# Two chunks inverted one by one, x ordered on chip, four raw weight buffers

## Chip, cores and metric

One core of a Trainium2 chip runs the whole program. The metric is the device time of one execution in microseconds (us); lower is better. Times of before: 2066.8 us, the median of 3 runs (2065.63 to 2069.86).

## What is computed

Three stages in fp32. A delta-rule attention over 768 steps for 4 x 8 heads of dimension 48, a mixture of 8 experts whose weights P come from 8 rounds of row and column normalisation over all tokens, and a gated product with an output matrix:

```python
for t in range(S):
    y[:, :, t] = einsum('bhd,bhde->bhe', q[:, :, t], state)
    v_old = einsum('bhde,bhd->bhe', state, kn[:, :, t])
    state = state + bt * einsum('bhd,bhe->bhde', kn[:, :, t], v[:, :, t] - v_old)
...
P = exp(x @ w_gate - max)
for _ in range(8):
    P /= P.sum(1, keepdims=True) + 1e-09
    P /= P.sum(0, keepdims=True) + 1e-09
    P *= N / E
out = sum over e of P[:, e:e+1] * (maximum(x @ w1[e], 0) @ w2[e])
...
y = ((x @ w1) * (x @ w2) @ w3) @ w_out
```

x is 3072 tokens of 384 features; an expert has 1024 hidden units.

## The kernel before

**Attention in 12 chunks of 64 steps.** Within a chunk the recurrence becomes a triangular system: the gram matrix of the keys of each head (64 x 64) is inverted, and the chunk is then a chain of small matmuls. 32 heads of a chunk lie side by side as 16 groups on two halves of the partitions. `prep_k(c)` loads keys, takes norms and the gram; `invert(j)` inverts for the chunks 2j and 2j+1 together, on VectorE (DVE), after a 32 x 32 transpose that brings heads into the partitions; `tt_make` makes the 64 x 64 inverse from 32 x 32 blocks. `prep_q(c)` makes q times k (tile `pt`). `seq(c)` is the chain over chunks: `um` (matmul into u), `um2` (the state), `pu` (the output of the chunk).

**The first two chunks are done differently**, to start early. For j = 0 only the diagonal 16 x 16 blocks are inverted, both chunks in one go (32 x 32 tiles with two blocks), and `substitute(c)` and three rounds of matmuls (`b<-vs,xst`, then twice `b<-u,xst`, with an add on DVE after each) replace the rest of the inverse.

**Expert 0 runs under the attention.** When a chunk's output x is there, `e0(c)` runs expert 0 on its 256 tokens: 72 matmuls `b<-xr,wA` and 72 `b<-hA,wA`, each 128x256. `seq(c)` writes x from `xst` to memory (`xs_d`), `xload` reads it back in another order of rows, ScalarE (ACT) rounds it into `xr`, and GpSimd (POOL) or DVE subtracts for the low half. `load_w(n)` brings the 8 blocks of expert 0's weights through two raw buffers (`yr`, `wraw`); ACT rounds a block into `wA` and POOL subtracts 768 columns for its low half. Logits of a chunk (`b<-xr,wg`, `b<-masks,yr`) follow. Then come the normalisation, experts 1 to 7 (phase B) and the last stage (phase C), from about 423 us on.

**What sets the order.** A planner (`Plan.order`) lists all operations before anything runs, by priorities, its own costs and ring buffers; each engine's list is then fixed and worked in order. TensorE (PE) gets fillers, dummy matmuls `b<-wz`, wherever the planner sees a gap before expert 0 starts. VectorE and GpSimd instructions that the planner marks `port=True` may hold each other up. All DMAs named here are issued by SyncE (SP), one after another.

Of the kernel before, what the change touches and what calls it, by code (L numbers as in the profile page):

```python
# [7 lines left out]
F32 = mybir.dt.float32  # L8
# [41 lines left out]
SUB = 2  # L50
FLAT = "p a b c d -> p (a b c d)"
# [28 lines left out]
class Plan:  # L80
# [58 lines left out]
    WARM = 20.0  # L139
    SEED = 32  # L140
    PASS_BY = .05
# [238 lines left out]
class Kernel:  # L380
# [56 lines left out]
    def setup(self):  # L437
        nc, T, g = self.nc, self.T, self.g
        n = NCH * NG
        self.open("const", "left", ones=((128, 128), F32), masks=((128, 78), F32),  # L440
                  wgr=((128, 3, NE), F32), p=((128, NTT + 1, NE + 1), F32),
                  rs=((128, NTT), F32), cs=((128, NE), F32), sml=((128, 8), F32))
        self.open("wg", "left", wg=((128, 3, 2 * NE), F32R), padl=((128, 24), F32))
# [13 lines left out]
                  asys=((128, 1056), F32), t=((128, 1056), F32), prod=((128, NP, 1024), F32), xs=((128, 256), F32), bm2=((128, 2, 32), F32), wz=((128, 384), F16),  # L457
# [52 lines left out]
    def prep_k(self, c):  # L510
# [13 lines left out]
        if st:  # L524
            n0 = [("n0", 0), ("n0", 1)]
            bm = lambda: T["bm"][:, 32 * j:32 * j + 32]
            nv = lambda: T["nv"][:, 32 * j:32 * j + 32]
            g.op({"DVE": .1}, lambda e: nc.vector.tensor_scalar(out=nr(0), in0=nr(0), scalar1=1e-30, scalar2=None, op0=ALU.max), w=n0, prio=pr)
            g.op({"ACT": .25}, lambda e: nc.scalar.activation(out=nr(1), in_=nr(0), func=AF.Sqrt), r=n0, w=["n1"], prio=pr)

            def newton(e):
                v = nc.vector
                v.reciprocal(out=nr(2), in_=nr(1))
                v.tensor_tensor(out=nr(2), in0=nr(2), in1=nr(0), op=ALU.mult)
                v.tensor_tensor(out=nr(1), in0=nr(1), in1=nr(2), op=ALU.add)
                v.tensor_scalar(out=nv(), in0=nr(1), scalar1=0.5, scalar2=1e-6, op0=ALU.mult, op1=ALU.add)
                v.reciprocal(out=nr(2), in_=nv())
                v.tensor_tensor(out=bm(), in0=bm(), in1=nr(2), op=ALU.mult)
                v.tensor_tensor(out=bm(), in0=bm(), in1=nr(2), op=ALU.mult)
            g.op({"DVE": 1.77}, newton, port=True, r=n0 + ["bm"], w=["n1", ("bm", j), ("nv", j)], prio=pr)  # L540
# [4 lines left out]
        if c < SUB:  # L545
            g.op({"POOL": .4}, lambda e: nc.gpsimd.memset(self.rb(c)[:, :, :, 48:64], 0.0), w=[("gm", c)], prio=-6)
# [7 lines left out]
        for hf in range(2):  # L554
# [33 lines left out]

    def invert(self, j):
        nc, g, T = self.nc, self.g, self.T  # L590
# [16 lines left out]
        for i in range(1, 8):  # L607
            pb = self.pring.new()
            pv = lambda pb=pb, i=i: T["prod"][:, pb.at, :4 * i * i].rearrange("p (b c q) -> p b c q", b=4, c=i)
            g.op({"DVE": dve(4 * i * i) + .12}, port=True, fn=lambda e, pv=pv, i=i: self.tt(  # L610
# [3 lines left out]
            g.op({"DVE": dve(4 * i * i) + .11}, lambda e, pv=pv, i=i: nc.vector.tensor_reduce(  # L614
# [30 lines left out]
        if j == 0:  # L645
            g.op({"DVE": 1.85}, lambda e: nc.vector.transpose(
                out=av().rearrange("p s i -> p i s"), in_=tm().rearrange("p c i -> p i c")),
                r=["t", ("t8", 0), ("t8", 1), ("tr", 0), ("tr", 1)], w=ka, prio=-131)
            for i in range(2):
                g.op({"ACT": .18}, lambda e, i=i: self.copy("ACT", T["bm2"][:, i], T["bm"][:, 0:32], T["masks"][:, (74, 64)[i]:(75, 65)[i]]),  # L650
                     r=[("bm", 0), "masks"], w=[("bm2", i)], prio=pr)
            for c in range(SUB):
                self.substitute(c)
            if SUB == 2:
                return
        rk = ["asys", "t", ("t8", 0), ("t8", 1)]
        by_rows(0, 16, 16, ["t", ("t8", 0), ("t8", 1), ("tr", 0), ("tr", 1)] + ([("s0", i) for i in range(2)] if j == 0 else []))
# [74 lines left out]
    def substitute(self, c):  # L732
# [5 lines left out]
        for i in range(2):  # L738
            g.op({"DVE": dve(512)}, port=True, fn=lambda e, i=i: self.tt(
                e, T["tt"][:, tt.at].rearrange("p h m t -> p (h m) t")[:, :, 32 * i:32 * i + 32], T["a0"][:, a0.at, 16 * c:16 * c + 16],  # L740
                T["bm2"][:, i, 16 * c:16 * c + 16].rearrange("p (s o) -> p s o", o=1).to_broadcast([128, 16, 32]), ALU.mult),
                r=[(a0, c, 0), (a0, c, 1), ("bm2", i)], w=[(tt, hf, i) for hf in range(2)] + [("s0", i)], prio=pr)
# [3 lines left out]
             r=[("gm", c)] + [(tt, hf, i) for hf in range(2) for i in range(2)], w=sr + [("gmr", c)], prio=pr)  # L746
        for hf in range(2):
            g.op({"ACT": act(512, True)}, lambda e, hf=hf: self.copy(e, self.rb(c)[:, hf], self.ps(sr[hf], 8, 64)),
                 r=[sr[hf], ("gmr", c)], w=[("R", c, hf)], prio=pr)

    def prep_q(self, c):
# [7 lines left out]
        sp = [self.psum.new("attn" if c else "early") for _ in range(2)]  # L759
# [7 lines left out]
        for hf in range(2):  # L767
            s, pt = sp[hf], self.PT[c, hf]
            raw = c < 2
            if raw:  # L770
                g.op({"ACT": act(512, True)}, lambda e, s=s, pt=pt: self.copy("ACT", T["pt"][:, pt.at // 2, pt.at % 2], self.ps(s, 8, 64)),
                     r=[s], w=[pt], prio=1.25 + c / 100)
# [14 lines left out]

# [829 lines left out]
```

## Time and profile before

| what | us |
|---|---|
| median of 3 runs | 2066.8 |
| the profiled execution, its own time | 2066.21 |
| its span, first to last instruction | 2064.1 |
| PE busy in the span | 2040.8 |
| first matmul of expert 0 starts at | 62.53 |

A row of the timeline gives the start, the duration, the engine with line and operation, the tile written and those read, the shape, how many instructions are merged, and in brackets the idle time before it with what ended it. `b` is a PSUM bank.

### The profile page before, as it was taken

How to read it: one execution, taken by the hardware profiler on the slowest of the kernel's cores; microseconds unless marked ns; L12 is line 12 of the kernel's file. 1: busy time of each engine (PE TensorE's matmuls, PEld its weight loads, DVE VectorE, ACT ScalarE, POOL GpSimd, SP SyncE). 2: the span in 40 equal slices, each digit the busy share in tenths (PEclk: the TensorE clock that was granted, in tenths of full speed). 3: DMA queues.
4: the chain of work that ended last, by engine and by line, in shares of the span. 5: the costliest groups of instructions: out<-in, count | busy, mean ns of one | idle time of the engine just before them, and what ended most of it. 6: DMA issues, size and time to landing. Idle time of an engine off the chain costs nothing.

```text
span 2064.1 us, 39972 instructions
## 1 busy us (share of the span) xinstructions
PE 2040.8 (99%) x16463; PEld 1748.6 (85%) x16463; DVE 1219.1 (59%) x1951; ACT 733.3 (36%) x1438; POOL 788.3 (38%) x845
## 2 busy tenths in 40 slices
PE   7999999999999999999999999999999999999999
PEld 6998999978888888888888888888888888988888
DVE  7998982765444545876666668767666743222222
ACT  6545433343443443422332333323323322222222
POOL 1300011067666667354455444444564544200000
PEclk9999999999999999999999999999999999999999
DMA  6444323276645546855654555755645637400000
GB/s 216 141 138 132 106 75 113 69 263 232 228 175 189 211 178 219 284 178 173 236 193 169 206 176 184 251 185 187 225 160 198 217 109 205 97 31 16 16 25 22
DMA packets 166614, 331.64 MB, mean 161 GB/s; under 512 B 13408, under 2 KB 117792, under 8 KB 154912
## 3 DMA queue, kind: packets, MB, share of 16 engines
q1 hardware_dynamic: 132544, 193.82, 27.8%
q0 software_dynamic: 33888, 135.28, 19.1%
q8 instruction: 129, 2.11, 0.4%
q14 instruction: 53, 0.43, 0.1%
HBM read 235.10 MB, written 93.95 MB: 159 GB/s over the span
## 4 chain that ended last, share of the span: by engine, by line
PE 93%; DVE 4%; DMA 1%; issue 1%; ACT 0%; SPq 0%; POOL 0%; DVEq 0%; POOLq 0%; ACTq 0%
PE b L402 93%; DVE prod L413 1%; DMA kt<-in_kT 0%; DVE xs L626 0%; SPq L433 0%; DMA xs_d<-xst 0%; DMA rawB<-in_moe_w 0%; DVE pt L413 0%; DVE t L626 0%; DMA xst<-xs_d 0%; DMA kn<-in_kn 0%; DVE tt L413 0%; DVE cv L413 0%; DVE hA L416 0%; DVE asys L600 0%
## 5 line engine op out<-in xcount | busy, mean ns | idle before, releaser
L402 PE MATMUL b<-hA,wA 128*128 128x512 f32 (+1 forms) x2367 | 506.5, 352 | 0.0
L402 PEld LDWEIGHTS b<-hA,wA 128*128 128x128 f32 x2367 | 391.8, 189 | 61.2
L413 POOL TENSOR_TENSOR acc<-acc,tmp 128x512 f32<-128x512 f32 x252 | 334.7, 1329 | 222.5 <-DVE tmp L413 221.2
L402 PE MATMUL b<-hB,wA 128*128 128x512 f32 x1521 | 386.2, 389 | 0.0
L402 PEld LDWEIGHTS b<-hB,wA 128*128 128x128 f32 x1521 | 285.5, 188 | 59.3
L402 PE MATMUL b<-xr,wA 128*128 128x256 f32 (+1 forms) x1620 | 326.0, 335 | 0.0
L402 PEld LDWEIGHTS b<-xr,wA 128*128 128x128 f32 x1620 | 250.2, 189 | 31.9
L406 ACT ACTIVATE rt<-b 128x512 f32<-128x512 f32 x300 | 178.7, 598 | 262.3 <-PE b L402 256.1
L402 PE MATMUL b<-xT,wA 128*128 128x512 f32 x1008 | 250.1, 389 | 1.8 <-POOL wA L413 1.8
L413 DVE TENSOR_TENSOR b<-b,rt 128x512 f32<-128x512 f32 x252 | 172.8, 694 | 106.2 <-ACT rt L406 73.7
L402 PEld LDWEIGHTS b<-xT,wA 128*128 128x128 f32 x1008 | 189.0, 188 | 41.8 <-POOL wA L413 2.6
L402 PE MATMUL b<-xT,wS 128*128 128x512 f32 x756 | 199.3, 390 | 1.2 <-ACT rt L406 1.2
L413 POOL TENSOR_TENSOR cv<-cv 128x256 f32<-128x256 f32 (+3 forms) x175 | 128.7, 735 | 177.3 <-DVE cv L1377 96.3
L413 DVE TENSOR_TENSOR tmp<-b,pb 128x512 f32<-128x512 f32 x150 | 103.3, 689 | 137.0 <-PE b L402 128.8
L416 DVE SCALAR_TENSOR_TENSOR hA<-b,hA 128x512 fp32r<-128x512 f32 x215 | 144.0, 687 | 61.7 <-ACT hA L942 30.5
L402 PEld LDWEIGHTS b<-xT,wS 128*128 128x128 f32 x756 | 141.7, 188 | 31.7 <-ACT rt L406 2.1
L413 DVE TENSOR_TENSOR rt<-b,rt 128x512 f32<-128x512 f32 x48 | 33.2, 692 | 186.0 <-PE b L402 186.0
L416 DVE SCALAR_TENSOR_TENSOR hB<-b,hB 128x512 fp32r<-128x512 f32 x169 | 114.2, 684 | 30.6 <-ACT hB L1182 30.3
L413 DVE TENSOR_TENSOR tmp<-b,yr 128x512 f32<-128x512 f32 x102 | 70.2, 689 | 97.5 <-PE b L402 92.8
L1182 ACT ACTIVATE hB<-b 128x512 fp32r<-128x512 f32 x169 | 100.3, 597 | 76.1 <-DVE b L413 73.8
L413 POOL TENSOR_TENSOR wA<-rawB,wA 128x768 fp32r<-128x768 f32 (+1 forms) x49 | 88.5, 1818 | 97.6 <-DMA pb<-p_d 72.1
L1182 ACT ACTIVATE hA<-b 128x512 fp32r<-128x512 f32 x167 | 97.4, 598 | 68.8 <-DVE b L413 42.2
(189 smaller groups left out, 2365.1 us busy)
## 6 DMA issues: line engine op xcount, KB each, us to landing
wA<-wq_d POOLq DMA_DIRECT2D x56, 1536.0 KB, 9.3
wq_d<-wA SPq DMA_DIRECT2D x28, 1536.0 KB, 6.9
wS<-ws_d POOLq DMA_DIRECT2D x56, 512.0 KB, 4.8
rawB<-in_moe_w SPq DMA_DIRECT2D x108, 192.0 KB, 3.1
ws_d<-wS SPq DMA_DIRECT2D x28, 512.0 KB, 6.3
w_d<-cv SPq DMA_DIRECT2D x112, 128.0 KB, 1.8
cvr<-in_w3T SPq DMA_DIRECT2D x32, 256.0 KB, 2.6
wS<-w_d POOLq DMA_DIRECT2D x32, 256.0 KB, 3.6
```

The costliest lines, as they stand in the source:

```text
L402: self.nc.tensor.matmul(*args, skip_group_check=True, **kw)
L406: self.nc.scalar.activation(out=out, in_=in_, func=AF.Copy, **({} if scale is None else {"scale": scale}))
L413: self.E[eng].tensor_tensor(out=out, in0=in0, in1=in1, op=op)
L416: self.nc.vector.scalar_tensor_tensor(out=out, in0=in0, scalar=scalar, in1=in1, op0=op0, op1=op1)
L1182: g.op({"ACT": actb(512)}, lambda e: nc.scalar.activation(out=hv(0), in_=self.ps(s, 512), func=AF.Relu), r=[s], w=[(out, 0, 0)], prio=pe)
```

## The change

- `blocks16(c)` is new: the 16 x 16 blocks of one chunk are scaled, transposed, inverted and transposed back by themselves; chunk 0 no longer waits for chunk 1's keys. Norms are taken per chunk for j = 0. The gram goes whole into `xst` (2 copies of 512 columns in place of 6 of 128), and the mask is applied on DVE after `substitute`'s matmuls.
- x is put into order on the chip: six DMAs of 16 partitions from `xst` to `xst`, with the rows of the first-layer and gate weights permuted on the host to match. The write to `xs_d` stays for the later passes; the read back goes.
- Weight blocks 2 and 3 of expert 0 take a `kraw` and a `vs` buffer, the loads of blocks 0 to 3 come earlier (`WP`), and POOL's subtraction is cut into three pieces of 256 columns.
- Three settings of the planner (`WARM`, `SEED`, `PASS_BY`) and some priorities. Pads grow with the new tiles.

```diff
+WP = (-11, -8, 5, 5)
...
-    WARM = 20.0
-    SEED = 32
-    PASS_BY = .05
+    WARM = 13.0
+    SEED = 26
+    PASS_BY = 0.02
...
-        if st:
-            n0 = [("n0", 0), ("n0", 1)]
...
+        if st or j == 0:
+            cs = slice(16 * st, 16 * st + 16) if j == 0 else slice(0, 32)
...
+            if j == 0:
+                g.op({"DVE": .2}, port=True, fn=lambda e: self.tt(
+                    e, T["bq"][:, :, cs], bm().rearrange("p (o s) -> p o s", o=1).to_broadcast([128, 6, 16]),
+                    T["masks"][:, 78:84].rearrange("p (q o) -> p q o", o=1).to_broadcast([128, 6, 16]), ALU.mult),
+                    r=[bk, "masks"], w=[("bq", st)], prio=pr)
...
+            if c < SUB:
+                g.op({"ACT": act(512, True)}, lambda e, s=s, hf=hf: self.copy("ACT", self.rb(c)[:, hf], self.ps(s, 8, 64), -1.0),
+                     r=[s], w=[("gm", c, hf)], prio=.5 if c == 0 else 1.3)
...
+    def blocks16(self, c):
...
+        g.op({"DVE": dve(512)}, port=True, fn=lambda e: self.tt(
+            e, v4(), v4(), T["bq"][:, 4:6, 16 * c:16 * c + 16].rearrange("p a (s o) -> p s a o", o=1).to_broadcast([128, 16, 2, 16]), ALU.mult),
+            r=[("bq", c)], w=ka, prio=pr)
+        g.op({"DVE": 1.0}, lambda e: nc.vector.transpose(
+            out=raw().rearrange("p i (a s) -> p i a s", a=2), in_=v4().rearrange("p s a i -> p i a s")), r=ka, w=["asys"], prio=pr)
+        g.op({"DVE": dve(256)}, port=True, fn=lambda e: self.tt(
+            e, am().rearrange("p i q -> p q i"), raw()[:, :, 0:16], raw()[:, :, 16:32], ALU.add), r=["asys"], w=[("F", c)], prio=pr)
+        for i in range(1, 8):
...
     def invert(self, j):
+        if j == 0:
+            for c in range(2):
+                self.blocks16(c)
+                self.substitute(c)
+            return
...
         for hf in range(2):
-            g.op({"ACT": act(512, True)}, lambda e, hf=hf: self.copy(e, self.rb(c)[:, hf], self.ps(sr[hf], 8, 64)),
-                 r=[sr[hf], ("gmr", c)], w=[("R", c, hf)], prio=pr)
+            g.op({"DVE": dve(512)}, lambda e, hf=hf: self.tt(
+                e, self.rb(c)[:, hf], self.ps(sr[hf], 8, 64), T["masks"][:, 84:148].rearrange("p (o t) -> p o t", o=1).to_broadcast([128, 8, 64]),
+                ALU.mult), r=[sr[hf], ("gmr", c), "masks"], w=[("R", c, hf)], prio=pr)
...
-        for b in range(2):
-            self.dma(lambda b=b: T["xs_d"][c].rearrange("h (j q e) t -> q e (h j) t", q=2, e=D)[b],
...
+        for k_ in range(3):
+            for b in range(2):
+                r0, r1 = 64 * b + 16 * k_, 64 * b + 48
+                self.dma(lambda r1=r1, k_=k_: xv()[r1:r1 + 16, :, k_], lambda r0=r0: xv()[r0:r0 + 16, :, 3], 16384,
+                         [(xb, 0), (xb, 1)], [(xb, "m", k_, b)], pr + .5, lat=.9, cost=.4)
...
+        for i in range(3):
+            g.op({"POOL": pool2(256)}, port=True, fn=lambda e, i=i: self.tt(
+                e, self.wb(n)[:, 768 + 256 * i:1024 + 256 * i], rv()[:, 256 * i:256 * i + 256],
+                self.wb(n)[:, 256 * i:256 * i + 256].bitcast(F32), ALU.subtract),
+                r=[(raw, 0), (raw, 1), ("w", sl, 0), ("t16e", 0)], w=[("w", sl, 1)], prio=prio)
```

DVE's list where the inversion for j = 0 starts; `asys` and `t` (now `t_119`) are its work tiles, `bq` holds the scales of chunk 0's blocks. Before:

```order
10 L539 TENSOR_TENSOR bm<-bm,nrm 128x32
11 L600 STREAM_TRANSPOSE asys<-a_113 128x1024
12 L602 STREAM_TRANSPOSE a_113<-bm 128x32
13 L413 TENSOR_TENSOR asys<-asys,a_113 128x1024
14 L413 TENSOR_TENSOR prod<-t,asys 128x4
15 L614 TENSOR_REDUCE t<-prod 128x4
```

The same place in the change:

```order
10 L545 TENSOR_TENSOR bm<-bm,nrm 128x16
11 L414 TENSOR_TENSOR bq<-bm,masks 128x6x16
12 L414 TENSOR_TENSOR a_113<-a_113,bq 128x512
13 L616 STREAM_TRANSPOSE asys<-a_113 128x512
14 L414 TENSOR_TENSOR asys<-asys 128x16x16
15 L414 TENSOR_TENSOR prod<-t_119,asys 128x2
16 L626 TENSOR_REDUCE t_119<-prod 128x2
```

The chunk's own 512 columns are scaled and transposed where 1024 of both chunks were; the same series comes a second time, for chunk 1, further down.

SP's list around the first x. Before, x goes to memory and back:

```order
30 L433 DMA vs<-in_v 128x768
31 L433 DMA xs_d<-xst 48x8x128 x2
32 L433 DMA yr<-in_moe_w 128x3x128
33 L433 DMA yr<-in_moe_w 128x384
34 L433 DMA kraw<-in_k 128x768
35 L433 DMA xst<-xs_d 128x6x128
```

And in the change:

```order
31 L434 DMA kraw<-in_k 128x768
32 L434 DMA xst<-xst 16x2x128 x6
33 L434 DMA kraw<-in_k 128x768
34 L434 DMA vs<-in_v 128x768
35 L434 DMA kt<-in_kT 128x1024
36 L434 DMA xs_d<-xst 128x3x128 x2
```

Six small DMAs within `xst` stand where two writes and one read stood.

PE's list between the first chunks and chunk 2; `asys,g` and `tt,g` are the first matmuls that use the inverse of chunks 2 and 3, `pt,u` (`pu`) comes later. Before:

```order
797 L402 MATMUL b_140<-hA,wA 128x256 x6
798 L402 MATMUL b_139<-tt,g_112 32x32 x16
799 L402 MATMUL b_140<-hA,wA 128x256 x9
800 L402 MATMUL b_142<-xr,wg 16x256 x3
801 L402 MATMUL b_142<-xr,wg 8x256 x3
```

In the change:

```order
757 L403 MATMUL b_144<-xr,wg 16x256 x3
758 L403 MATMUL b_144<-xr,wg 8x256 x3
759 L403 MATMUL b_138<-xr,wA 128x256 x9
760 L403 MATMUL b_141<-hA,wA 128x256 x12
761 L403 MATMUL b_144<-masks,yr 128x8 x2
762 L403 MATMUL b_144<-asys,g_112 32x32 x16
763 L403 MATMUL b_138<-xr,wA 128x256 x15
```

Expert 0 has moved ahead of chunk 2: counted over the list, 282 of the 288 matmuls of expert 0 for chunks 0 and 1 stand before chunk 2's `pu`, where it was 183. The last 1830 rows of PE's list, from the end of the attention on, are the same in both.

## Rows read from the trace of the kernel before

**Rows 1.** The page: busy time of each engine, its share of the span, instructions.

```profile
PE 2040.8 (99%) x16463; PEld 1748.6 (85%) x16463; DVE 1219.1 (59%) x1951; ACT 733.3 (36%) x1438; POOL 788.3 (38%) x845
```

**Rows 2.** Windows by stage: length, busy us (instructions) of PE, PEld, DVE, ACT, POOL; clock.

```profile
0.00:62.50 62.50, 50.77 (x1336) 43.40 (x1337) 48.85 (x91) 42.87 (x116) 16.30 (x20) 1.00 0.65 224
62.50:77.70 15.20, 15.20 (x375) 13.84 (x373) 15.17 (x16) 7.31 (x17) 7.40 (x4) 1.00 0.37 111
77.70:125.00 47.30, 46.55 (x1238) 42.69 (x1237) 42.24 (x72) 22.98 (x56) 2.66 (x3) 1.00 0.39 117
...
423.00:2064.00 1641.00, 1636.19 (x7389) 1375.76 (x7389) 891.28 (x1409) 536.81 (x981) 731.67 (x789) 1.00 0.49 169
```

**Rows 3.** PE by line and form from 0 to 62.5 us: the fillers.

```profile
L402 PE MATMUL b<-wz 128*128 128x256 f16 x184 | 25.0, 293 | 0.0
```

**Rows 4.** Timeline of PE up to the first matmul of expert 0.

```profile
15.23 2.32 PE L402 MATMUL b<-wz 128*128 128x256 f16 x10
18.43 2.22 PE L402 MATMUL b<-kt 48*64 48x64 f32 x64 [0.89 <-ACT pt L406]
20.59 4.84 PE L402 MATMUL b<-wz 128*128 128x256 f16 x28
25.36 1.16 PE L402 MATMUL b<-kt 48*64 48x64 f32 x64
26.45 3.23 PE L402 MATMUL b<-wz 128*128 128x256 f16 x28
...
48.75 1.11 PE L402 MATMUL b<-pt,u 64*48 64x64 f32 x64
...
62.53 0.68 PE L402 MATMUL b<-xr,wA 128*128 128x256 f32 x3
```

**Rows 5.** Timeline of ACT and SP: the way of chunk 0's x.

```profile
49.90 1.09 ACT L406 ACTIVATE xst<-b 128x512 f32<-128x512 f32 x2 [2.50 <-PE b L402]
...
59.90 0.85 ACT L406 ACTIVATE xr<-xst 128x768 fp32r<-128x768 f32 x1 [2.08 <-DMA xst<-xs_d]
...
51.01 0.85 SPq L433 DMA_DIRECT2D xs_d<-xst  x2
```

**Rows 6.** DMA issues by line: KB each, median us to landing.

```profile
kraw<-in_k SPq DMA_DIRECT2D x12, 384.0 KB, 4.2
...
y_d<-yr SPq DMA_DIRECT2D x36, 128.0 KB, 2.1
...
p_d<-tmp SPq DMA_DIRECT2D x2, 48.0 KB, 1.6
```

**Rows 7.** Timeline of DVE: the inversion for j = 0, and that for j = 1.

```profile
13.14 1.93 DVE L600 STREAM_TRANSPOSE asys<-a 128x1024 f32<-128x1024 f32 x1
...
28.26 1.29 DVE L413 TENSOR_TENSOR tt<-a,bm 128x512 f32<-128x512 f32 x2
...
33.09 1.80 DVE L522 TENSOR_REDUCE nrm<-kn 128x16 f32<-128x768 f32 x2
...
86.39 2.03 DVE L673 STREAM_TRANSPOSE a<-t 128x1024 f32<-128x1024 f32 x1
```

**Rows 8.** Timeline of DVE and POOL: one form of DVE beside POOL, and alone.

```profile
52.18 3.67 DVE L413 TENSOR_TENSOR prod<-asys,t 128x512 f32<-128x512 f32 x2
...
115.00 1.29 DVE L413 TENSOR_TENSOR prod<-asys,t 128x512 f32<-128x512 f32 x2
...
42.14 1.81 POOL L413 TENSOR_TENSOR wA<-wraw,wA 128x768 fp32r<-128x768 f32 x1 [0.61 <-ACT wA L406]
...
53.05 2.26 POOL L413 TENSOR_TENSOR wA<-wraw,wA 128x768 fp32r<-128x768 f32 x1
```

**Rows 9.** Timeline of PE and DVE at chunks 2 and 3.

```profile
112.90 1.11 PE L402 MATMUL b<-pt,u 64*48 64x64 f32 x64
...
139.39 0.96 DVE L413 TENSOR_TENSOR xr<-xst,xr 128x768 fp32r<-128x768 f32 x1 [0.76 <-ACT xr L406]
```

**Rows 10.** Waits of PE: us in total, times, longest.

```profile
PE b L402 <- DVE u L413: 3.1, 2, 2.5
```

More of the change, by code (lines that the diff above doesn't have):

```diff
@@ L523, in prep_k @@
              r=[kn], w=[("n0", st)], prio=pr)
-        if st:
-            n0 = [("n0", 0), ("n0", 1)]
[L526 to L529, printed above, removed]
+        if st or j == 0:
+            cs = slice(16 * st, 16 * st + 16) if j == 0 else slice(0, 32)
+            n0 = [("n0", x) for x in range(2) if j or x == st]
+            n1 = [("n1", x) for x in range(2) if j or x == st]
+            bm = lambda: T["bm"][:, 32 * j:32 * j + 32][:, cs]
+            nv = lambda: T["nv"][:, 32 * j:32 * j + 32][:, cs]
+            nq = lambda i: nr(i)[:, cs]
+            g.op({"DVE": .1}, lambda e: nc.vector.tensor_scalar(out=nq(0), in0=nq(0), scalar1=1e-30, scalar2=None, op0=ALU.max), w=n0, prio=pr)
+            g.op({"ACT": .25}, lambda e: nc.scalar.activation(out=nq(1), in_=nq(0), func=AF.Sqrt), r=n0, w=n1, prio=pr)
@@ L539, in newton @@
-                v.tensor_tensor(out=bm(), in0=bm(), in1=nr(2), op=ALU.mult)
-            g.op({"DVE": 1.77}, newton, port=True, r=n0 + ["bm"], w=["n1", ("bm", j), ("nv", j)], prio=pr)
+                v.reciprocal(out=nq(2), in_=nq(1))
+                v.tensor_tensor(out=nq(2), in0=nq(2), in1=nq(0), op=ALU.mult)
+                v.tensor_tensor(out=nq(1), in0=nq(1), in1=nq(2), op=ALU.add)
+                v.tensor_scalar(out=nv(), in0=nq(1), scalar1=0.5, scalar2=1e-6, op0=ALU.mult, op1=ALU.add)
@@ L644, in invert @@
                  lambda p=p: xt(p, 8), 8, 8, 8, [("tr", p), ("x8", p)], [("t8", p)])
[L645 to L655, printed above, removed]
         rk = ["asys", "t", ("t8", 0), ("t8", 1)]
-        by_rows(0, 16, 16, ["t", ("t8", 0), ("t8", 1), ("tr", 0), ("tr", 1)] + ([("s0", i) for i in range(2)] if j == 0 else []))
+        by_rows(0, 16, 16, ["t", ("t8", 0), ("t8", 1), ("tr", 0), ("tr", 1)])
         x16 = lambda: xt(0, 16).rearrange("p c q -> p q c")
@@ L758, in prep_q @@
         k = self.K[c]
-        sp = [self.psum.new("attn" if c else "early") for _ in range(2)]
+        sp = [self.psum.new("attn" if c > 1 else "early") for _ in range(2)]
         for hf in range(2):
@@ L801, in scale @@
                     self.copy("ACT", va()[:, x], va()[:, x], T["nv"][:, 16 * c + x:16 * c + x + 1])
-            g.op({"ACT": .8}, scale, r=[("nv", 0)], w=[vk[i // 2]], prio=1.2 + c)
+            g.op({"ACT": .8}, scale, r=[("nv", 0, c)], w=[vk[i // 2]], prio=1.2 + c / 5)
         if j:
@@ L806, in seq @@
                 r=[("nv", j)], w=vk, prio=10.0 * j + .5)
-        kr = self.kraw.new()
+        kr = self.slots0[c][1] if j == 0 else self.kraw.new()
         self.dma(lambda: T["kraw"][:, kr.at].rearrange("p g d -> p (g d)"), lambda: self.a["k"][c], 393216, [], [kr], 10.0 * j - 16.8 if j else -15.9 + c)
@@ L829, in seq @@
                     V(hf), self.ps(sk[hf], 8, D), -1.0, V(hf), ALU.mult, ALU.add), r=[sk[hf]], w=[(v, hf)], prio=pr)
-        sy = two()
+        sy = two() if c else [self.psum.new("early") for _ in range(2)]
         if c > 0:
@@ L1587, in layouts @@
     masks[:, 64] = i >= 32
-    for b in range(3):
-        masks[:, 75 + b] = -1.0 * (i >= 16 * b + 16)
+    for b in range(4):
+        masks[:, 78 + b] = i // 16 == b
+    for b in range(2):
+        masks[:, 82 + b] = i % 32 // 16 == b
+    masks[:, 84:148] = i[:, None] // 16 < t[None, :] // 16
     masks[:, 66:74] = i[:, None] % NE == t[None, :NE]
@@ L1592, in layouts @@
                masks=masks, w3T=f(inputs["moe2_w3"].T).view(np.int64))
+    p = np.arange(128)
+    q, e = p // 64, p % 64
+    rows = np.concatenate([np.where(e < D, D * (2 * n + q) + e, D * (6 + q) + 16 * n + e - D) for n in range(3)])
     for nm in ("moe_w_gate", "moe_w1", "moe_w2", "moe2_w1", "moe2_w2", "moe2_w_out"):
         res[nm] = f(inputs[nm])
+        if nm in ("moe_w_gate", "moe_w1"):
+            res[nm] = f(np.take(inputs[nm], rows, axis=-2))
         if nm.startswith("moe2"):
```

125 lines of the change are left out of this document (78 added, 47 removed).

## Prediction

> **What bounds the kernel now.** I read the page's shares first: PE is busy for 2040.8 us, 99% of the span [rows 1]. Then the windows by stage, to see where a change at the start can act at all. From 423 us on PE works 1636.2 of 1641.0 us [rows 2], on a list that the change leaves as it is, so the end moves by what is won or lost before that. From 62.5 us on PE is full too (15.2 of 15.2 us, then 46.6 of 47.3) [rows 2]: expert 0 fills all holes of the attention. Only the first 62.5 us are loose: PE looks busy for 50.8 of them, but 25.0 us of that are fillers [rows 2, 3]. So the quantity to follow is PE's useless time: fillers, idle time and matmuls at the lower clock level. What the change takes from it, the program gains, as long as later stages don't give it back.
>
> How much there is: before 62.53 us PE does 15 groups of 64 small matmuls, about 1.07 us each when the engine runs at full level (a gram starting at 25.36 ends after 1.16 with some overlap) [rows 4], and three rounds of 2.07 us, together 22.2 us. The other 40.3 us are useless. Two things are seen in them. At 18.43 a group took 2.22 us, at 25.36 the same form 1.16 [rows 4]: the engine is at its 1.2 GHz level first and at 2.4 GHz after steady fillers. And chunk 0's chain is long: DVE's inversion of both chunks takes from 13.14 to 28.26 [rows 7], `pu` of chunk 0 comes at 48.75 and the first matmul of expert 0 only 13.8 us later, at 62.53 [rows 4], after the write to memory and the read back [rows 5].
>
> **The change, part by part.** *When expert 0 starts.* PE's new list has 37 fillers after the two q-k groups, then the gram of chunk 2, 7 fillers and chunk 0's substitution. In before the fillers began at 15.23 right behind the same q-k groups; I keep that. At the lower level ten fillers took 2.32 us, across the rise 28 took 4.84, at full level 28 took 3.23 [rows 4]. The first 37 cross the rise, at 4.84 / 28 = 0.173 each 6.4 us: 21.6. The gram adds 1.1, seven fillers 0.8: the substitution can start at 23.5. DVE is ready by then: chunk 0's norm no longer waits for chunk 1, and its half-size inversion I add up to 9.3 us (scale 0.65, transpose half of 1.93, an add 0.45, seven steps 3.3, two products with their sums 2.8, transpose back 1.05) from about 10.3, so 19.6 against 28.26 [rows 7]. From the substitution to the first matmul of expert 0 PE's list holds 99 fillers at 3.23 / 28 = 0.115 [rows 4] (11.4 us) and 13.5 us of useful groups: 23.5 + 24.9 = 48.4 us, if nothing in between is late.
>
> The other chain to that point: `pu` would end at about 40, two copies 1.09 [rows 5], six issues of SP at about 0.38 each (two took 0.85 [rows 5]) 2.3, the last landing, ACT's 0.85 [rows 5], DVE's subtraction 0.96 [rows 9], which POOL did for chunk 0. No row shows a DMA from SBUF to SBUF. Nearest are 48 KB in 1.6 us and 128 KB in 2.1 [rows 6]; I take 1.9, with 1.6 below and twice 2.1 above. Sum about 47.1, just inside PE's own 48.4. I add 0.6 for DVE operations held up by POOL and put the start at 49.0. Until then PE has done 12 groups and three rounds, 18.9 us. Useless: 49.0 - 18.9 = 30.1, against 40.3. **Gain 10.2.**
>
> *Fillers after the start.* Of 190 fillers in before, 184 lay ahead of 62.5 us [rows 3]; in the change 18 come after the first matmul of expert 0 (1, 16 and 1): 12 more at 0.115. **Loss 1.4.**
>
> *Chunk 1's rounds.* In before, matmuls of expert 0 stood between them; now the second and third round stand back to back, and each has to wait for DVE's add with whatever stands in front of it. Chunk 0's rounds in before waited 3.1 us in two places, 2.5 of it behind DVE operations that POOL held up [rows 10]. Between none and those 3.1 I take 1.9, since DVE's list has a product or a sum of 0.6 to 1.2 us in front of three of the four adds. **Loss 1.9.**
>
> *Chunk 2's x.* This is the place where the gain is paid back. Before chunk 2's `pu` (112.90 in before [rows 9]) PE's list now has 282 of the 288 matmuls of expert 0 that exist by then; before it was 183. Behind `pu` there is little left: 6 matmuls, chunk 3's two state groups, its `um` and a gram, 5.1 us. x takes longer: `pu` 1.1, copies 1.1, issues 2.3, landing 1.9, 0.85 and 0.96, that is 8.2, which by the read-back way was 13.8. PE waits 8.2 - 1.1 - 5.1 = 2.0, and some sequencing; I take 2.3. Before lost 0.7 in the same stretch (47.30 less 46.55 [rows 2]). **Loss 1.6.**
>
> The later chunks I count at nothing: by the lists expert 0 still has work waiting when their x comes (at chunk 4's logits 0.67 chunks' worth, 1.33 in before), so neither the shorter way of x nor a DVE that is a little later shows. The larger `masks` load, the gram copies, the loads of four weight blocks before 20 us cost nothing as long as SP and ACT reach them ahead of the matmuls of blocks 2 and 3, which PE reaches after 53. The pads keep the tile offsets at multiples of 128 bytes where they were already: zero.
>
> Sum: -10.2 + 1.4 + 1.9 + 1.6 = -5.3 us. The profiled execution took 2066.2 us around its span of 2064.1, 0.6 below the median of 2066.8, so the span goes to about 2058.8 and the time to 2066.8 - 5.3 = **2061.5 us**.
>
> **The margin that decides.** DVE is the engine that can take it all. In before, DVE needed 53.3 us from 33.09 to the start of the transpose at 86.39 that ends the inversion for chunks 2 and 3 [rows 7]. Its list there at undisturbed durations: two instructions of 512 columns take 1.29 us, the second starting 0.6 after the first [rows 8], so eight of those 4.8 and twelve of 1024 columns at about 1.13 13.6; twelve adds for u 5.6, fourteen small steps 3.8, transposes 4.0, norms 4.6, the rest 4.9, together 41.3. So 12 us were holds and waits. One such hold: two products took 3.67 us beside POOL's 2.26 us subtraction, and 1.29 when POOL was still [rows 8]. In the change DVE has more to do from the masked R of chunk 0 (about 25.8) to that transpose: the same 41.3 less a norm, and in addition chunk 1's inversion (9.3), a norm of 1.8, chunk 1's two `tt` and two masks (2.4), four `pt` or masks more, two subtractions for `xr`, two halves for expert 0 and a scale of `vs` (some 7), by the list 61 us: 86.8 without any hold. PE reaches the first matmul that needs it at 49.0 + 48 + 1.9, about 99. So DVE may lose 12 us in holds and waits and no more, which is just what it lost before. Every further microsecond is one of PE.
>
> A rule of the Trainium skill bears on this (SBUF — State Buffer, "Who interferes with whom"): a VectorE instruction with two SBUF inputs and a GpSimd instruction that reads SBUF exclude each other for a whole instruction. The 2.4 us of that hold agree with it. By the rule each of the 24 new pieces can hold DVE once, which is the first rival below.
>
> **Rivals.** *DVE's holds eat the gain.* POOL's 24 pieces at a third of 1.81 [rows 8] plus overhead, about 0.65 each, could each hold DVE: 15.6 us at the worst, against about 9 us of holds in before. With 3 us of waits on others that is 18.6, 6.6 more than the 12 that are free: 2061.5 + 6.6 = 2068, no change. For it: 24 chances in place of 8, and small steps of 0.2 us that fit between pieces of 0.65. Against: pieces are shorter, and a sum of 0.6 us, which was not held, hides one.
>
> *Slower.* The same mechanism with one step more: if DVE loses over 22 us between 26 us and the transpose, PE waits 10 us at the first matmul of chunks 2 and 3, and the time is 2071 or more. It decides from 21.5 us of holds on.
>
> *The x way does not shorten.* If the six DMAs land one after the other behind `kraw`'s 384 KB, at 4.2 us [rows 6] as the upper bound, chunk 0's start moves to 51.3, and chunk 2's wait grows by the same 2.3: the gain is 0.8, time 2066.
>
> *More than forecast.* If DVE keeps up and chunk 2's x finds PE still busy, only the fillers come off: 10.2 - 1.4 = 8.8, 2058; with chunk 0 at its floor of 48.4 it is 2057.4.
>
> **How the numbers follow.** A difference under 0.2% (4.1 us) can't be told from none here. The forecast, a gain between 4.1 and 8: 0.46. More: 0.13. Holds or the x way leave it within 4.1 us: 0.28. Slower: 0.13. That makes 0.59, 0.28 and 0.13. The range from 2055.5 (floor for chunk 0, no waits, DMA at 1.6) to 2069 (the first rival with a microsecond more) leaves some 2 in 10 out; the forecast's own range is 2058.5 to 2063.
>
> **What would show it.** Right: the first `xr,wA` group between 47.5 and 50.5, `pu` of chunk 2 between 113 and 120 with 282 matmuls of expert 0 behind it; a PE wait of 1.5 to 3 us for `xr` right after. Wrong: a first group after 52; waits of PE on DVE `asys` or `u` of over 5 us in all; a chain that runs through DVE for more than 10 us between 50 and 110 us; x DMAs that land later than 3 us.

## The result: 1.4% slower, most of it behind the part that was edited

The changed kernel takes 2099.1 us (median of 6 runs) beside 2069.5 of before, a ratio of 1.0141 with a 95% interval of 1.0116 to 1.0167. The forecast was 2061.5, faster. The medians of before lie between 2070.7 and 2075.0 in the later comparisons, so runs are compared by their ratio to before, measured on the same chip.

The page of the changed kernel, beside [rows 1] (PEld is PE's weight load):

```profile
PE 2066.3 (99%) x16434; PEld 1753.0 (84%) x16434; DVE 1227.3 (59%) x1978; ACT 729.6 (35%) x1425; POOL 794.7 (38%) x866
```

The way of chunk 0's x and the first matmul of expert 0, from the timeline of all engines, beside [rows 4, 5]:

```profile
41.13 1.08 ACT L407 ACTIVATE xst<-b 128x512 f32<-128x512 f32 x2
42.30 4.44 SPq L434 DMA_DIRECT2D xst<-xst  x6
49.33 0.84 ACT L407 ACTIVATE xr<-xst 128x768 fp32r<-128x768 f32 x1 [3.21 <-DMA xst<-xst]
...
50.21 0.96 DVE L414 TENSOR_TENSOR xr<-xst,xr 128x768 fp32r<-128x768 f32 x1 [3.18 <-ACT xr L407]
...
50.23 0.39 PE L403 MATMUL b<-xr,wA 128*128 128x256 f32 x1 [0.88 <-ACT xr L407]
```

Expert 0 starts at 50.23 where it was 62.53. The windows of the changed kernel by stage (length, then busy us and instructions of PE, PEld, DVE, ACT, POOL, granted clock, DMA share, GB/s):

```profile
0.00:48.00 48.00, 39.84 (x1093) 34.73 (x1094) 35.32 (x83) 34.19 (x90) 14.46 (x29) 1.00 0.68 236
48.00:62.53 14.53, 13.05 (x264) 11.59 (x265) 11.02 (x18) 8.83 (x22) 2.91 (x4) 1.00 0.70 237
62.53:100.00 37.47, 34.84 (x760) 31.84 (x752) 35.24 (x53) 10.31 (x22) 3.99 (x6) 1.00 0.24 75
100.00:125.00 25.00, 24.66 (x726) 22.35 (x729) 19.76 (x45) 13.02 (x33) 1.95 (x3) 1.00 0.25 78
125.00:150.00 25.00, 20.03 (x605) 18.67 (x597) 22.53 (x28) 11.23 (x25) 0.00 (x0) 0.80 0.38 105
150.00:200.00 50.00, 47.18 (x1243) 43.79 (x1245) 46.10 (x73) 24.51 (x61) 9.21 (x6) 1.00 0.38 116
...
423.00:2064.00 1641.00, 1638.71 (x7268) 1357.68 (x7267) 897.20 (x1410) 535.06 (x977) 735.87 (x793) 1.00 0.49 170
```

Two things are off. Between 125 and 150 us PE idles 5 us, at a mean clock of 0.80; in before PE was busy for all of it:

```profile
125.00:150.00 25.00, 25.00 (x694) 22.87 (x693) 23.65 (x29) 12.64 (x28) 1.37 (x2) 1.00 0.38 117
```

And from 423 us on, in the same 1641 us and on the same list, PE is as full as before but gets through 7268 instructions where it did 7389 [rows 2]. Of the 32.5 us between the two profiled spans (2096.6 and 2064.1) 25.1 come from there: on the chain of work that ended last, the long pieces of PE begin at 423.30 us in before and at 430.73 in the changed kernel, 7.4 us later, and the rest is lost behind that.

PE by line and form from 430 to 2060 us, changed kernel (busy us, mean ns of one):

```profile
L403 PE MATMUL b<-hB,wA 128*128 128x512 f32 x1521 | 393.3, 394 | 0.0
L403 PE MATMUL b<-hA,wA 128*128 128x512 f32 x1503 | 386.1, 392 | 0.0
L403 PE MATMUL b<-xT,wA 128*128 128x512 f32 x990 | 245.6, 390 | 0.0
...
L403 PE MATMUL b<-xT,wS 128*128 128x512 f32 x744 | 201.1, 396 | 0.9 <-ACT rt L407 0.9
L403 PE MATMUL b<-xr,xT 128*128 128x512 f32 x432 | 99.9, 390 | 0.0
L403 PE MATMUL b<-wS,xT 128*128 128x512 f32 x363 | 85.1, 395 | 0.0
```

In before all these forms took 389 or 390 ns:

```profile
L402 PE MATMUL b<-hB,wA 128*128 128x512 f32 x1521 | 386.2, 389 | 0.0
L402 PE MATMUL b<-hA,wA 128*128 128x512 f32 x1503 | 381.6, 389 | 0.0
...
L402 PE MATMUL b<-xT,wS 128*128 128x512 f32 x738 | 194.4, 390 | 1.2 <-ACT rt L406 1.2
```

The single matmul has become slower, at full clock, and not every form alike: those that read one tile of the pools opened on the left (`wA`, `xT`, `xr`, `hA`) and one of the right (`hB`, `wS`) by 5 to 6 ns; of those with both tiles left, `hA` with `wA` by 3, `xT` with `wA` and `xr` with `xT` by 0 or 1. The change moved the left tiles by 384 bytes (`masks` and `padl` grew); `hB`, `wS` and `acc` stand where they stood. In before `wA` begins at byte 18816 of a partition, `hB` at 170880 and `wS` at 203648, multiples of 256 bytes apart.

### The profile page after: what moved, and what is told of

It reads as the page before. It is cut to its first block, busy times and chain, and to the rows that moved or that the text cites. A ratio compares the mean times of both kernels' runs of the same rounds, so it can differ in the third digit from the quotient of the medians.

```text
span 2096.6 us, 40059 instructions
## 1 busy us (share of the span) xinstructions
PE 2066.3 (99%) x16434; PEld 1753.0 (84%) x16434; DVE 1227.3 (59%) x1978; ACT 729.6 (35%) x1425; POOL 794.7 (38%) x866
## 4 chain that ended last, share of the span: by engine, by line
PE 93%; DVE 3%; DMA 2%; SPq 1%; ACT 1%; issue 1%; POOL 0%; ACTq 0%; POOLq 0%; DVEq 0%
PE b L403 93%; SPq L434 1%; DMA rawB<-in_moe_w 0%; DVE prod L414 0%; DMA xst<-xst 0%; DMA qt<-in_qT 0%; POOL sums L414 0%; DVE t L689 0%; DMA kt<-in_kT 0%; DVE acc L414 0%; DVE tt L414 0%; DMA pb<-p_d 0%; DVE cv L414 0%; ACT xst L407 0%; DMA acc<-in_moe_w 0%
## 5 line engine op out<-in xcount | busy, mean ns | idle before, releaser
L403 PE MATMUL b<-hB,wA 128*128 128x512 f32 x1521 | 393.3, 394 | 0.0
L403 PE MATMUL b<-xr,wA 128*128 128x256 f32 (+1 forms) x1620 | 332.3, 339 | 4.2 <-DVE hA L417 1.0
L403 PE MATMUL b<-xT,wS 128*128 128x512 f32 x756 | 204.4, 396 | 0.9 <-ACT rt L407 0.9
```

The source lines that it names most:

```text
L403: self.nc.tensor.matmul(*args, skip_group_check=True, **kw)
```

## The experiments

**Where the tiles lie.** Theory P says that the place does it. e1 gives the changed kernel 128 bytes more pad, so that the left tiles lie 512 bytes from their old place; e2, e3 and e4 shift the left tiles of the kernel before.

```diff
e1 (of the changed kernel)  -padl=((128, 48), F32)   +padl=((128, 80), F32)
e2, e3, e4 (of before)      -padl=((128, 24), F32)   +padl=((128, 120 | 56 | 88), F32)
```

> The changed kernel with padl 48 -> 80: the tiles wA, hA, xr, yr, xT and all others of the left side begin 128 bytes later, 512 bytes later than in the kernel before in place of 384, and so at the same distance modulo 512 bytes from wS, hB and acc, which did not move. Every engine's list of instructions is that of the changed kernel, word for word. Theory P (placement: the 25 us lost behind 430 us come from where the two operands of a matmul begin relative to one another): median 2071 to 2077, b<-hB,wA back at 389 ns and b<-xT,wS at 389, the stretch behind the last chunk back at 1641 us. Theory L (they come from the edits themselves: other timing of transfers, the reordered rows of weights): 2097 to 2101, b<-hB,wA at 393.

> The kernel before with padl 24 -> 120 and nothing else: the left tiles begin 384 bytes later, as in the changed kernel. The lists of instructions are those of before. Theory P: 2092 to 2097, b<-hB,wA at 393 and b<-xT,wS at 395 where they were at 389, attention still over near 423 us. Theory L: 2066 to 2072, all at 389.

> The kernel before with padl 24 -> 56: left tiles 128 bytes later, so wA and hB are 128 bytes apart modulo 512 with the sign the other way. Theory P, if only an odd number of 128-byte units between the operands costs: 2092 to 2097. Theory P, if it is the one distance of the changed kernel that costs (or the tile's own address): 2066 to 2072. Theory L: 2066 to 2072.

> The kernel before with padl 24 -> 88: left tiles 256 bytes later, an even number of 128-byte units. Theory P with a period of 256 bytes: 2066 to 2072, b<-hB,wA at 389. Theory P with a period of 512 bytes or more: slower, up to 2097. Theory L: 2066 to 2072.

Then the right tiles are moved (`padr` 24 to 56), with the left ones and alone:

> The kernel before with padl 24 -> 56 and padr 24 -> 56: the left tiles begin 128 bytes later and the right ones (wS, hB, acc, rawB) 128 bytes earlier, so they are again a multiple of 256 bytes apart, but all now at an address that is a multiple of 256 (before: all 128 past one). Lists unchanged. Theory P-relative (what counts is the distance between left and right tiles): no change, ratio 0.998 to 1.002, b<-hB,wA at 389 ns. Theory P-absolute (a tile at a multiple of 256 bytes is read more slowly): as slow as the run with left tiles alone shifted or slower, ratio 1.010 or more, b<-hB,wA at 393 or more, and b<-xT,wA, both of whose tiles are left, no faster than 390.

> The kernel before with padr 24 -> 56 alone: the right tiles begin 128 bytes earlier, the left ones stay. Lists unchanged. Theory P-relative: ratio 1.008 to 1.013, b<-hB,wA at 393 and b<-xT,wS at 396 as with the left tiles shifted. Theory P-absolute: only forms with a right tile slow, ratio 1.003 to 1.009, and b<-hA,wA (no right tile) stays at 389.

| run | left, right moved from before (bytes) | distance of left and right, modulo 256 | ratio to before | `hB,wA`, ns | first `hB,wA` at, us | from there to the end, us |
|---|---|---|---|---|---|---|
| changed kernel | +384, 0 | 128 | 1.0141 | 394 | 439.1 | 1657.5 |
| e1 | +512, 0 | 0 | 1.0023 [1.0008, 1.0038] | 389 | 441.3 | 1634.1 |
| e2 | +384, 0 | 128 | 1.0110 [1.0084, 1.0137] | 393 | 440.3 | 1657.9 |
| e3 | +128, 0 | 128 | 1.0095 [1.0064, 1.0127] | 393 | 437.9 | 1657.8 |
| e4 | +256, 0 | 0 | 0.9985 [0.9964, 1.0006] | 389 | 434.3 | 1632.7 |
| e5 | +128, -128 | 0 | 0.9994 [0.9977, 1.0011] | 389 | 442.0 | 1633.7 |
| e6 | 0, -128 | 128 | 1.0111 [1.0090, 1.0132] | 393 | 446.2 | 1657.0 |

The last two columns are read from the traces; in before the first `hB,wA` starts at 431.6, and 1632.5 us follow. The lists of all engines are the same within each family, so nothing but the place differs. What counts, of the places tried, is the distance between left and right tiles modulo 256 bytes, not the address of either (e5). From the first `hB,wA` on, the four placements at 0 take 1632.5 to 1634.1 us and the four at 128 take 1657.0 to 1657.9. Of the 1.41% some 1.2 go with e1. The forms of e1, to be set beside those above:

```profile
L403 PE MATMUL b<-hB,wA 128*128 128x512 f32 x1521 | 386.2, 389 | 0.0
L403 PE MATMUL b<-hA,wA 128*128 128x512 f32 x1503 | 382.1, 389 | 0.0
L403 PE MATMUL b<-xT,wA 128*128 128x512 f32 x990 | 245.0, 389 | 0.0
...
L403 PE MATMUL b<-xT,wS 128*128 128x512 f32 x747 | 197.0, 390 | 1.2 <-ACT rt L407 1.2
```

**What is left: the attention.** With the tiles in place the changed kernel is still 0.23% (some 5 us) above before, though expert 0 starts 13.7 us earlier (48.8 in e1). This rests on the medians (e7 and e13, below, repeat it). A single trace doesn't show it: with before's own list the first `hB,wA` came anywhere from 431.6 to 442.0 even where its matmuls were fast (e4, e5), and 441.3 in e1 lies in that range. The timeline of PE in the changed kernel where the hole is:

```profile
122.27 1.11 PE L403 MATMUL b<-pt,u 64*48 64x64 f32 x64
123.31 0.98 PE L403 MATMUL b<-hA,wA 128*128 128x256 f32 x6
124.22 1.15 PE L403 MATMUL b<-st,kt 48*64 48x48 f32 x64
125.19 1.08 PE L403 MATMUL b<-qt,st 48*48 48x64 f32 x64
128.18 1.92 PE L403 MATMUL b<-vs,tt 64*64 64x48 f32 x64 [1.92 <-issue]
133.15 1.99 PE L403 MATMUL b<-kt 48*64 48x64 f32 x64 [3.06 <-DMA kt<-in_kT]
135.07 1.01 PE L403 MATMUL b<-xr,wA 128*128 128x256 f32 x3
```

After six last matmuls of expert 0 at 123.31 PE has only the bare chain of the chunks, until chunk 2's x is there, 12.8 us after its `pu` began. SP's queue in the same stretch:

```profile
124.53 4.44 SPq L434 DMA_DIRECT2D xst<-xst  x6
129.07 0.53 SPq L434 DMA_DIRECT2D kt<-in_kT  x1
```

The six transfers cost SP 0.74 us each, and the load of `kt` that PE waits for stands behind them. What idling does to the clock is seen in windows of 2 us (PE's busy time with its matmuls, granted clock, DMA share, GB/s):

```profile
125.00:127.00 2.00, 1.26 (x91) 1.00 0.04 8
127.00:129.00 2.00, 0.82 (x36) 0.91 0.12 25
129.00:131.00 2.00, 1.10 (x40) 0.50 0.55 87
131.00:133.00 2.00, 0.00 (x0) 0.50 1.09 305
133.00:135.00 2.00, 1.85 (x64) 0.50 0.76 213
135.00:137.00 2.00, 2.00 (x59) 0.50 1.02 345
137.00:139.00 2.00, 2.00 (x35) 0.53 0.43 92
139.00:141.00 2.00, 2.00 (x31) 1.00 0.44 169
```

Behind 4 us in which it was busy for 2.1, PE drops to the 1.2 GHz level (0.50) and stays there until about 138.7: 6.95 us busy between 129 and 139, worth some 3.5 at full level. The hole costs 5.0 us and, as an estimate, up to 3.5 more.

*e7* moves that load ahead of the transfers, *e8* takes back the new way of x:

```diff
e7 (of e1)  +order.remove(self.KL[7])
            +order.insert(order.index(self.XM[2, 0, 0]), self.KL[7])
e8 (of e1)  seq, xload and the rows of the weights as in the kernel before
```

> The changed kernel with padl 80 (the placement of before), and one DMA issue moved on SP's list: the load of chunk 7's kt stands ahead of the six transfers of chunk 2's x, not behind them. Nothing else on any engine's list. Theory K (the rest of the loss is one stall: SP waits for chunk 2's xst, the kt load that PE needs for a gram at 129 us stands behind it, PE idles 4.3 us and then works 10 us at half the clock): that stall and the clock level of 0.5 between 129 and 139 us are gone, 8 to 10 us less than e1, ratio to before 0.996 to 0.999. Theory H (VectorE, busy 22.5 of 25 us there, is the bound; the wait moves to its next result and the clock falls anyway): no more than 3 us less than e1, ratio 1.000 to 1.004, and PE waits over 3 us for DVE between 125 and 200 us.

> The changed kernel with padl 80, and x ordered as before (written to memory in two transfers, read back in one; weight rows not reordered); all else as changed, the planner's order made anew. Theory X (the on-chip way carries the earlier start): first b<-xr,wA at 54 to 57 us in place of 49, time 3 to 8 us above e1. Theory K (the six transfers on SP cost more than the shorter way gives): no stall for kt near 129 us, no level of 0.5 there, time 3 to 8 us below e1.

e7: 1.0025 [1.0010, 1.0040], no better than e1; theory K in this form fell. The load went out at 126.59 in place of 129.07, and could not go earlier: its buffer is that of chunk 3, whose last matmul on it ends just then. The wait for `kt` was gone, but x's transfers, now behind the load, began at 127.01 in place of 124.75, PE waited for ACT's `u` (1.8 us) and for `issue` (1.8) instead, and the clock fell to 0.50 all the same. Theory H's ratio came, its waits for VectorE didn't (1.8 us in all between 125 and 200). e8: 1.0037 [1.0025, 1.0049], the first `xr,wA` at 53.2 in place of 48.8, the time the same as e1's within the intervals: neither theory's 3 to 8 us came. If the new order that e8 also got did nothing, 4.4 us of earlier start were worth next to nothing.

Theory D then put the loss on VectorE, whose inversion for chunks 2 and 3 ends at 100.7 in e1 and at 88.4 in before [rows 7]. Four kernels with an order made anew:

```diff
e9  (of before)  x ordered on chip as in the change, nothing else
e10 (of e1)      -for i in range(1, 8):   +for i in range(1, 8 if c == 0 else 1):   (and the two products)
e11 (of e1)      -SEED = 26               +SEED = 32
e12 (of e9)      load_w, its rings and WP as in the change
```

> The kernel before with one part of the change alone: x ordered on chip (six transfers, two writes after them, weight rows reordered); masks, pads, inversion of both chunks in one go and planner constants as before; the planner's order made anew. Theory D (VectorE paces the chain of the chunks, and inverting chunks 0 and 1 one by one puts 12 us more of VectorE's list ahead of the inversion for chunks 2 and 3, so every later chunk's x comes later and PE runs out of expert 0's work): without the one-by-one inversion the first b<-xr,wA comes at 56 to 59 us, VectorE's last transpose for chunks 2 and 3 still ends at 87 to 90, chunk 2's x is copied at 112 to 116, PE waits less than 5 us between 62 and 200 us, ratio to before 0.9960 to 0.9985. Theory X (six issues on SP and what waits behind them cost more than the shorter way gives): waits of PE for kt or xr of over 4 us after 62 us, ratio 1.000 to 1.004.

> The changed kernel with padl 80, leaving out work: of chunk 1's 16 x 16 inversion the seven product steps with their sums and the two products of 512 columns with theirs (18 VectorE instructions, 8.3 us in e1); order made anew. Theory D: the last transpose for chunks 2 and 3 ends near 92 us in place of 100.7, chunk 2's x is copied 6 to 9 us earlier than in e1 (123.6), PE's waits between 100 and 250 us shrink by half, 5 to 10 us less than e1, ratio 0.9975 to 1.0000. Theory S (PE runs out of expert-0 work because it starts early, whatever VectorE does): within 3 us of e1, ratio 1.001 to 1.004.

> The changed kernel with padl 80 and the planner's SEED back at 32 (the changed kernel has 26): the same operations in another order drawn by the planner. It tells how far a newly drawn order alone moves the time. Theory D: within 4 us of e1 either way, with the same late chain (last transpose for chunks 2 and 3 at 98 to 103 us). Rival (the loss is one unlucky order): 5 us or more below e1.

> As the run with x ordered on chip alone, and with a second part of the change: four raw weight buffers and POOL's subtractions in 24 pieces of 256. Theory D: VectorE loses little by it, within 3 us of the run with x alone, ratio 0.9950 to 0.9985. Theory H (POOL's 24 pieces hold VectorE's two-input instructions, which is what delays the chain): the last transpose for chunks 2 and 3 ends over 4 us later than in the run with x alone, and the time is 3 to 8 us above it.

All four are slower: 1.0090 [1.0068, 1.0112], 1.0075 [1.0050, 1.0100], 1.0088 [1.0064, 1.0112], 1.0075 [1.0051, 1.0098]. In e10 the first links of D came true (last transpose at 93.4, chunk 2's x copied at 115.4 in place of 123.6), but chunk 3's x then came at 152.6, 11 us later than in e1, and PE idled 7.3 us between 150 and 175, 4.1 of it in one wait for `kt`. In e9 the inversion for chunks 2 and 3 ended at 101.4, though chunks 0 and 1 were inverted in one go. e12, with POOL's 24 pieces, ended it at 88.9 and was not above e9, so nothing points at POOL's pieces. And e11 shows that another draw of the same operations takes 1.0023 to 1.0088. These runs can't carry a verdict on one edit, so the next four change one thing on an unchanged list, but for the last (some lines are shortened):

```diff
e13 (of e7)      chunk 1's 18 VectorE instructions of e10 are not issued; the order stays
e14 (of before)  +for _ in range(12): tensor_reduce(out=dum, in_=asys[:, 0:512])   ahead of the transpose for j = 1
e15 (of e7)      the transfers with b = 1 (three of six) are issued by ACT, not by SP
e16 (of before)  -SEED = 32   +SEED = 26
```

> The kernel of e7 (changed kernel, padl 80, chunk 7's kt ahead of chunk 2's x on SP), leaving out the 18 VectorE instructions of chunk 1's inversion as in e10, but without a new order: every other instruction stands where it stood in e7. Theory D (VectorE's list paces the chain): VectorE is 8 us ahead from 45 us on, its last transpose for chunks 2 and 3 ends near 92 us, PE's waits between 100 and 250 us fall from about 9 us to under 4, the half clock near 130 us is gone, 6 to 10 us less than e7, ratio to before 0.9975 to 0.9995. Theory L (the chain is paced by its own latencies on PE, ACT and the transfers, VectorE has room): within 3 us of e7, ratio 1.001 to 1.004.

> The kernel before with 12 VectorE sums of 512 columns added (0.69 us each by e1's rows, 8.3 us in all, into a tile that nobody reads) in front of the inversion for chunks 2 and 3; everything else stands where it stood. Theory D: the last transpose for chunks 2 and 3 ends at 96 to 97 us in place of 88.4, and from 100 us on PE waits for VectorE: 4 to 9 us more, ratio 1.002 to 1.0045. Theory L: under 2 us more, ratio 0.999 to 1.001.

> The kernel of e7, with three of the six transfers that order each chunk's x issued by ACT, right behind its copies, and three by SP; order of all else as in e7. Theory X (the six issues, 4.4 us on SP for chunk 2, are what makes x late): x is there about 2 us earlier in every chunk, 4 to 10 us less than e7, ratio 0.9975 to 1.000. Theory D: within 3 us of e7, ratio 1.001 to 1.004.

> The kernel before with the planner's SEED at 26 (the changed kernel's) in place of 32, nothing else: the same operations in another order. Theory O (the order drawn is what the attention part stands and falls with; both kernels were left at a good draw): 4 to 14 us more, ratio 1.002 to 1.007, with PE waits and half clock spread over 50 to 350 us. Theories D and X: within 3 us of before.

e13: 1.0022 [1.0006, 1.0037], as e7. VectorE, in the timeline of e13, won nothing by being 8 us lighter, because it stands at chunk 0's x:

```profile
40.57 2.44 DVE L414 TENSOR_TENSOR tt<-a,bq 128x512 f32<-128x512 f32 x2
46.54 0.56 DVE L417 SCALAR_TENSOR_TENSOR vs<-b,vs 128x384 f32<-128x384 f32 x1 [3.53 <-issue]
50.51 0.96 DVE L414 TENSOR_TENSOR xr<-xst,xr 128x768 fp32r<-128x768 f32 x1 [3.41 <-ACT xr L407]
...
53.92 2.02 DVE L668 STREAM_TRANSPOSE asys<-a 128x1024 f32<-128x1024 f32 x1
```

The transpose that opens the inversion for chunks 2 and 3 starts at 53.92, in e7 at 53.25. So chunk 1's 18 instructions are not what costs the 5 us, and theory D is out in that form. e14: 1.0050 [1.0033, 1.0066]; the added work also stood ahead of chunk 0's rounds, the first `xr,wA` came at 74.8 in place of 62.5, and the time rose by 10. Here a start that was 12.3 us later cost nearly its full length; the one that is 13.7 earlier in e1 gives nothing. e16: 1.0039 [1.0023, 1.0054], so before too loses 8 us with another draw.

e15: **0.9992 [0.9976, 1.0007]**, 0.33% (some 7 us) below e7, as theory X had it. The way of chunk 2's x in e7, on ACT and SP:

```profile
124.55 1.09 ACT L407 ACTIVATE xst<-b 128x512 f32<-128x512 f32 x2 [1.39 <-PE b L403]
...
127.01 4.70 SPq L434 DMA_DIRECT2D xst<-xst  x6
...
133.01 0.84 ACT L407 ACTIVATE xr<-xst 128x768 fp32r<-128x768 f32 x1 [5.99 <-DMA xst<-xst]
```

ACT and its queue, then SP's queue, in e15:

```profile
120.79 1.09 ACT L407 ACTIVATE xst<-b 128x512 f32<-128x512 f32 x2 [1.40 <-PE b L403]
...
122.79 0.61 ACTq L434 DMA_DIRECT2D xst<-xst  x1
...
123.46 1.31 ACTq L434 DMA_DIRECT2D xst<-xst  x2
127.76 0.84 ACT L407 ACTIVATE xr<-xst 128x768 fp32r<-128x768 f32 x1 [4.00 <-DMA xst<-xst]
```

```profile
122.83 0.33 SPq L434 DMA_DIRECT2D kt<-in_kT  x1
123.25 1.89 SPq L434 DMA_DIRECT2D xst<-xst  x3
```

The last transfer is on its way 3.3 us after the copies, in e7 6.1. Of these 2.8 us the landing takes some back: from the start of `pu` (119.65, in e7 123.40) to ACT's rounding of x into `xr` it is 8.1 us in place of 9.6. That x is there at 127.76 in place of 133.01 is for the most part older: `pu` itself starts 3.8 us earlier than in e7. The first `hB,wA` comes at 432.4, in e7 at 438.5, in before at 431.6. The Trainium skill (DMA: Bandwidth & Descriptors, "Issuing engines are not separate DMA queues") says that issuing from several engines saves only the time it takes to issue, which it calls usually small beside the transfer. The trace agrees that issue time is what was saved (4.70 us on SP, 1.89 with the rest on ACT), and here it was not small.

Two last kernels look for more: the six issues back to back on both queues, and three ready VectorE instructions ahead of the wait seen in e13.

```diff
e17 (of e15)  +order[i:i] = six[1:]      (right behind six[0], for every chunk)
e18 (of e17)  +order.insert(order.index(self.XD[0]), o)   for both pt masks of chunk 1 and the norm of chunk 3
```

> The kernel of e15 with each chunk's six transfers issued directly one after another, three by SP and three by ACT, so that no copy of ACT that waits for something else stands between them (in e15 ACT's third one for chunk 0 came 2.4 us late behind a copy that waited for wraw). Theory X: x of chunk 0 is there 1.5 to 2.5 us earlier, 1 to 4 us less than e15, ratio to before 0.997 to 0.999. If the x way is no longer what paces: within 1 us of e15, ratio 0.9985 to 1.000.

> The kernel of e17 with three VectorE instructions that are ready by then (both masks of chunk 1's pt, the norm sum of chunk 3; 2.2 us) put ahead of chunk 0's subtraction for xr, where VectorE idles for x. Theory V (VectorE's list, held by that wait, paces the later chunks): the last transpose for chunks 2 and 3 ends about 2 us earlier than in e17, the time is 1.5 to 4 us less, ratio 0.996 to 0.9985. Rival (VectorE has room there): within 1 us of e17.

0.9997 [0.9988, 1.0006] and 1.0000 [0.9986, 1.0013]: both as before and as e15. In e17 ACT copies chunk 0's x at 46.0 in place of 47.6, and nothing came of it; the last transpose ended at 96.8 and 98.0, no earlier in e18. Theory V was a miss. No version was found that beats the kernel before.

## Why the prediction was wrong

**The step that failed** is the sentence that PE works from 423 us on "on a list that the change leaves as it is, so the end moves by what is won or lost before that", with "the pads keep the tile offsets at multiples of 128 bytes where they were already: zero". The list did stay; the price of its entries did not. I had taken 128 bytes for the unit that counts, with no row behind it; e1 to e6 show that 256 is, in steps of 128. The term that was put at zero measured 1.0 to 1.2%, 20 to 25 us, four times the whole gain that was forecast.

**The gain at the start was right.** Forecast: expert 0 at 49.0, 10.2 us of useless PE time less. Measured: 50.2 in the changed kernel, 48.8 in e1; with the 18.9 us of useful work that I had counted, 31.3 us are useless at 50.2, 9.0 less than before. Its parts were not right, and that the start still came near is in part luck: x's chain, summed to 47.1 and hidden behind PE's own 48.4, is what the first matmul now waits for (0.88 us, on ACT's `xr`). An issue of SP takes 0.74 us (forecast 0.38, itself misread: the row cited, two in 0.85, gives 0.43), and from the end of the issues to ACT's copy it took 2.6 (forecast 1.9), so the way of x was 2.8 us longer than the 8.2 I had summed. The fillers I had priced by two clock levels before 25 us; that rests on the times of one form alone, as the granted clock that the profile gives there is 1.00.

**Chunk 2's x was seen and mis-sized.** A wait of 2.3 us was forecast behind its `pu`, 1.6 more than before lost, with 282 matmuls of expert 0 ahead. The place was right, though `pu` came at 122.3, past the 113 to 120 that I had named; there was a hole of 5.0 us, and then up to 3.5 us lost at the lower clock level. My sum had no term for the clock, although it had priced the fillers by it, nor for what stands behind the six issues on SP.

**"The later chunks I count at nothing" was near the mark; the first four were not.** From 48 to 423 us PE idles 16.4 us in the changed kernel, 6.7 in before (5.7 and 8.1 in e4 and e5, with the same list); even in e15 it is 14.6. Of the 9.7 us more, 4.1 lie between 48 and 100 us, where I had 1.9 for chunk 1's rounds, 5.0 in the hole, and 1.0 from 150 us on, with 0.4 less between 100 and 125. That takes back the 9.0 us of the start: the chain of the chunks does not come earlier with expert 0, `pu` of chunks 2 and 3 at 122.3 and 140.8 where it was 112.9 and 128.1. That expert 0's work is used up before the chain delivers is argued from this and from e14 and e15, not shown by a run of its own.

**VectorE's margin** was near the mark: its last transpose for chunks 2 and 3 started at 98.6 in the changed kernel, with about 99 worked out as the limit. The rivals built on it (holds by POOL) did not come about. Added up from the trace, VectorE's instructions with two inputs took 4.0 us more than at their shortest between 26 and 100.5 us; in before it was 9.3 between 33 and 88.4.

**Still open:** how the 5 us of e1 divide among the edits. e15 (which keeps e7's move) removes them, but every kernel whose order was drawn anew came out 0.4 to 0.9% above before (e8 to e12, e16), and the change brought a new draw with it.

## What to carry to other kernels

When tile sizes change, compare the mean time of each matmul form in stages that nobody touched, and compare the bytes between the tiles that matmuls read, modulo 256, before blaming the edit. An earlier start gains only as much as the work that it starts on can last until the next link of the chain, and a hole on PE can be paid twice, as the one at 127 us was, the second time by the clock. Transfers that are small in bytes can be long in issues: count them on the queue, with what stands behind them.

## What was not expected of the hardware

A 128 x 512 fp32 matmul took 389 ns or 393 to 396 ns depending on whether the tiles of the left and the right pools lay a multiple of 256 bytes apart or 128 bytes off that; over the 1640 us of full PE that made 20 to 25 us. The next matmul's weights count too: in the traces of the changed kernel, e2 and e6 an `xT,wA` that is followed by an `xT,wS`, whose weights come from the right, took 396 ns, and one followed by another `xT,wA` took 389 to 390; in before, e1 and e5 both took 389 to 390. `hA,wA` and `xr,wA`, with both tiles on the left, slowed by 3 to 4 ns as well, `xT,wA` and `xr,xT` on average by at most 1; why, no run here tells.
